# Transposing the backward weights in another order, and an f32 selection product in 32-column groups

## The chip, the cores and the metric

The kernel runs on one core of one Trainium2 chip. The metric is the device time of one execution in microseconds (us), given as the median of several runs. The engines named below are PE (matrix products and transposes; PEld are its weight loads), DVE (vector engine), ACT (scalar engine), POOL (GpSimd) and SP (SyncE, which here only issues DMAs). PE writes to PSUM, which holds eight banks of 2 KB per partition; DVE and ACT copy ("evict") results from there to SBUF.

## The reference

The function is the gradient of a sum of two branches behind a layernorm: a recurrent attention layer with 8 memory rows that are handed from one 32-row segment to the next, and an MLP with squared ReLU. All ten gradients are returned beside the output.

```python
for s in range(n_seg):                       # 64 segments of 32 rows
    h = jnp.concatenate([mem, xs], axis=1)   # 8 memory rows + 32 rows, D = 512
    q, k, v = (jnp.einsum('btd,dhe->bhte', h, W) for W in (Wq, Wk, Wv))   # 32 heads of 128
    scores = jnp.einsum('bhqe,bhke->bhqk', q, k) * scale
    p = _softmax(jnp.where(mask, scores, -1e9))
    o = jnp.einsum('bhqk,bhke->bhqe', p, v)
    o = jnp.einsum('bhte,hed->btd', o, Wo)
    mem = o[:, :M, :].copy()
    outs.append(o[:, M:, :])
# B: h = xn @ w1 + b1; out = relu(h)**2 @ w2 + b2
# out = x + A(xn) + B(xn);  the result is (out, vjp(grad_out) for x, mem0, Wq, Wk, Wv, Wo, w1, b1, w2, b2)
```

The inputs are bf16: x is 1 x 2048 x 512, Wq, Wk and Wv are 512 x 32 x 128, Wo is 32 x 128 x 512, w1 is 512 x 1792.

## The kernel before, in words

The program has four stages: the MLP, forward and backward, with the layernorm (to about 250 us); the forward recurrence (to about 1226 us, with a seam behind it); the backward recurrence (about 1312 to 2435); and the products that make the gradients of Wq, Wk, Wv and Wo (to the end).

In the first three stages nothing is issued in the order of the source. Each stage adds operations to a `_Plan` (L40): an engine or a choice of engines with an estimated duration, the keys that the operation reads and writes, a priority (0 for the recurrence, 1 for work beside it), and a latency. `run` (L100) gives each operation a rank, the longest path of estimated costs to the end, and then simulates the engines: it takes the operation that can start first, prefers a higher rank among those that can start at about the same time, adds `_TURN` (0.095 us) where PE changes between tile forms ("f" full 128x128, "w" 128x32 column groups, "d" 32x32 blocks), and writes out the order found. Every engine then works through its own list in this order, with semaphores between engines. A changed estimate, a new dependency or a changed priority can so move any operation of the stage.

`Stage.bank` (L348) hands out PSUM banks: each kind ("c", "f", "m" forward; "c", "r", "f" backward) is a ring of a fixed number of banks, and an operation that gets a bank depends on whatever used that bank before it in the source.

One segment of the forward recurrence is `chain` (L956): projections q, k, v, scores, softmax, products with v, product with Wo (`wo_part`), and the selection `tm` (L1001), eight bf16 matmuls that pick the memory rows out of `mb` for the next segment. Beside it run the memory rows' own work for each block of four segments (`l_proj`, `l_attn`) and `dw_unit` (L1056), which makes the gradients of w1 and w2 in 14 units of two 128-row chunks; each chunk is evicted into the single buffer `wt` and stored, 28 stores in all, on SP's queue. For w1's gradient the chunk is transposed once more through PSUM back into `wt` before it is stored.

The backward recurrence needs the weights transposed. `turn` (L361) does this for Wq, Wk or Wv in place in 16 groups: eight 128x128 PE transposes into one bank, one eviction of 128x1024. `turn_o` (L377) does it for Wo, also 16 groups, each with two evictions of 128x512. Wq (kind "m", two banks) and Wo (kind "c", four banks) are turned at the end of the forward plan (L1108, L1109), Wv and then Wk at the start of the backward plan (L1374), both with kind "f", two banks, which the memory rows' work of backward also uses.

One segment of the backward recurrence is `chain` (L1298), from segment 63 to 0: the product `gO` of the incoming gradient with Wo, its transposes `gOT`, `dP`, the softmax backward on DVE (L1163 to L1168), then three parts, each a product in 32x32 blocks (`d2`, `d1`, `d0`), an eviction to `dN`, a DVE transpose to `dT` and 64 matmuls of 128x512 (`dh_part`, L1172) with the transposed Wv, Wk and Wq. They add up in `ps_dRA`. DVE or ACT copies this to `R_A` (f32, 128 x 512) in two halves. The selection product `gm` (L1344) adds up the four 32-row groups of `R_A` and keeps the 8 memory rows, transposed: for each 128-column chunk `dc`, `R_A`'s chunk is the stationary operand (128x128, f32) and the constant `sel8` (128x8) the moving one. DVE copies the result into `gT` (L1349), which is the input of the next segment's `gO`. `l_pre` (L1190) makes the memory rows' gradients that `d2` (`gLN`) and `d1` (`dSL`) of a block need; `l_post` follows a block.

The last `l_attn` of forward (b = 15) takes part of its `VM` from SBUF, with four small DMAs issued by ACT (L914).

Of the kernel before, what the change touches and what calls it, by code (L numbers as in the profile page):

```python
# [17 lines left out]
P = 128  # L18
# [7 lines left out]
class _PE(dict):  # L26
    shape = None
# [8 lines left out]
class _Op:  # L36
    __slots__ = ("idx", "cost", "fn", "prio", "deps", "users", "left", "done", "end", "eng", "lat", "shape")


class _Plan:  # L40
# [11 lines left out]

    def add(self, cost, fn, R=(), W=(), prio=1, lat=None):
        o = _Op()
        o.idx = len(self.ops)
        o.cost = cost
# [43 lines left out]
    def run(self):  # L100
# [4 lines left out]
        for o in reversed(ops):  # L105
            c = min(o.cost.values())
            t = 0.0
            for u in o.users:
                same = o.cost.keys() == u.cost.keys() and "SP" not in o.cost
                t = max(t, rank[u.idx] + (0.0 if same else o.lat + _HOP))  # L110
            rank[o.idx] = c + t
        elig = [o for o in ops if o.left == 0]
# [74 lines left out]
def kernel(  # L187
# [152 lines left out]
    class Stage:  # L340


        def __init__(self, plan, pools):
            self.plan = plan
            self.pools = pools
            self.cnt = {k: 0 for k in pools}

        def bank(self, kind, shape, dt, name):  # L348
            n = self.pools[kind][1]
            key = (kind, self.cnt[kind] % n)  # L350
            self.cnt[kind] += 1
            return _Bank(self.pools[kind][0], key, shape, dt, name)

# [6 lines left out]

        def turn(self, kind, nm, reg, key, okey):  # L361

            for g in range(DC * NI // 2):
                dc, i0 = g % DC, 2 * (g // DC)
                blk = reg[:, dc, i0 * JQ * P:(i0 + 2) * JQ * P]
                bk = self.bank(kind, [P, 8, P], BF16, "ps_" + nm)

                def tr(e, blk=blk, bk=bk):
                    src = blk.rearrange("p (i m c) -> p i c m", i=2, c=JQ)
                    for i in range(2):  # L370
                        for c in range(JQ):
                            transpose_to(bk()[:, JQ * i + c, :], src[:, i, c, :])
                self.plan.add(pe(0.46, "f"), tr, [key] if g else [], [bk.key] + ([] if g else [key]), 1)
                self.evict(lambda blk=blk: blk, bk,
                           lambda bk=bk: bk()[:].rearrange("p k d -> p (k d)"), [(okey, g)], 1, {"DVE": 0.85, "ACT": 1.1})

        def turn_o(self, kind, nm, reg, key, okey):  # L377

            for g in range(2 * NI):
# [8 lines left out]
                self.plan.add(pe(0.46, "f"), tr, [key] if g else [], [bk.key] + ([] if g else [key]), 1)  # L388
                for d in range(2):
                    self.evict(lambda blk=blk, d=d0 + d: blk[:, :, d * P:(d + 1) * P].rearrange("p j (a c) -> p j a c", c=JQ), bk,  # L390
                               lambda bk=bk, d=d: bk()[:, d].rearrange("p c (j a) -> p j a c", j=JQ), [(okey, g, d)], 1, EV_B)

# [373 lines left out]
    with tc.tile_pool(name="fw", bufs=1) as fw, \  # L766
# [137 lines left out]
        def l_attn(b):  # L904
# [4 lines left out]
            else:  # L909
# [3 lines left out]
                for j in range(JQ):  # L913
                    sg.dma(lambda j=j: flat(VM)[32 * j + M * n:32 * (j + 1)], lambda j=j: flat(vN)[32 * j:32 * j + M],  # L914
                           [("vN", 0), ("vN", 1)] + ([("VMe", x) for x in range(JQ)] if j == 0 else []),
                           ["VM"] if j == 0 else [("VMx", j)], 0, eng="ACT")
            bk = sg.bank("f", [P, NI, 2 * RL], F32, "ps_scL")
# [138 lines left out]
        def dw_unit(which, u):  # L1056
# [59 lines left out]
    if True:  # L1116
# [181 lines left out]
        def chain(s):  # L1298
# [41 lines left out]
            if s > 0:  # L1340
                p1, v1 = ((s - 1) // SPB) % 2, (s - 1) % SPB
                bm = sg.bank("c", [P, DC, M], F32, "ps_gm")
                for hf in range(2):
                    def gm(e, hf=hf):  # L1344
                        for dc in (2 * hf, 2 * hf + 1):
                            nc.tensor.matmul(bm()[:, dc, :], lhsT=R_A[:, dc * P:(dc + 1) * P], rhs=sel8[:],  # L1346
                                             start=True, stop=True, skip_group_check=True)
                    A(pe(0.46, "f"), gm, [("R_A", hf)], [bm.key], 0)
                A({"DVE": 0.19}, lambda e: V.tensor_copy(gT[p1][:, :, RA * v1:RA * v1 + M], bm()[:]),  # L1349
# [211 lines left out]
```

## Time and profile before

| what | us |
|---|---|
| median of 3 runs | 3028.18 (3020.16 to 3029.71) |
| the profiled execution | 3031.71 |
| its span | 3029.9 |
| PE busy | 2788.3 |
| DVE busy | 1558.8 |
| ACT busy | 959.2 |
| POOL busy | 352.8 |
| stage 250 to 1226, forward recurrence | 976 |
| stage 1226 to 1312, the seam | 86 |
| stage 1312 to 2435, backward recurrence from the second segment | 1123 |

The profile is of one execution. "Busy" is the time in which at least one instruction of the engine is under way; matmuls overlap, and their ends are modelled. A row of a timeline or a group reads: start, duration, engine, line, operation, output<-inputs, shapes, number of instructions; in brackets the idle time of the engine just before it and what ended it. In a group's row the three durations are least, median and largest, in ns. The granted clock is the share of PE's full clock that was passed to it. A helper's line (L311, L315, L317, L359) stands for many places, so the tile's name tells them apart: `WA` holds Wq, Wk and Wv, `WB` Wo, `PA` the inputs of a segment, called `hA` forward and `gT` backward.

### The profile page before, as it was taken

Reading aid. Unit: us, or ns where it says so; the run is one execution under the profiler, and the core shown is the slowest. Engines: PE = TensorE matmul, PEld = TensorE weight load, DVE = VectorE, ACT = ScalarE, POOL = GpSimd, SP = SyncE. Lnnn points to the kernel's source line nnn. Section 1 sums busy time; section 2 is a strip of 40 time slices with the busy share of each in tenths; the row PEclk is TensorE's granted clock in tenths of the full one; section 3 lists DMA queues with packets and bytes.
Section 4 is the critical chain, followed back from the end, with each engine's and each line's share of the span. In section 5 each row is a group of like instructions: output and inputs, shape, how many; then the busy total and the mean of one; then the engine's idle time right before and its main releaser. Section 6 shows DMA issues by size and latency. Waiting matters only on the chain.

```text
span 3029.9 us, 129853 instructions
## 1 busy us (share of the span) xinstructions
PE 2788.3 (92%) x58168; PEld 1601.9 (53%) x58168; DVE 1558.8 (51%) x3378; ACT 959.2 (32%) x1978; POOL 352.8 (12%) x608
## 2 busy tenths in 40 slices
PE   8998999999999899888898898989899899999999
PEld 6664555555555555655555555555555544444444
DVE  5544555555555555655555555655655521332322
ACT  4324444444454444422333333333333310000000
POOL 1111111111111111100000000000000001211111
PEclk9999999999999999999999999999999999999999
DMA  6648665566555665456767777777777789788861
GB/s 208 219 141 228 167 170 174 170 174 179 161 153 164 159 173 173 130 139 187 206 201 204 206 204 196 220 209 200 208 214 214 197 288 310 235 256 277 248 182 44
DMA packets 551933, 589.96 MB, mean 195 GB/s; under 512 B 237445, under 2 KB 353078, under 8 KB 549198
## 3 DMA queue, kind: packets, MB, share of 16 engines
q1 hardware_dynamic: 537342, 530.72, 61.3%
q0 software_dynamic: 13968, 50.87, 4.9%
q8 instruction: 454, 7.44, 1.1%
q14 instruction: 105, 0.86, 0.1%
q10 hardware_dynamic: 64, 0.07, 0.0%
HBM read 283.32 MB, written 262.68 MB: 180 GB/s over the span
## 4 chain that ended last, share of the span: by engine, by line
PE 55%; issue 19%; DMA 10%; DVE 8%; SPq 3%; ACT 3%; POOL 2%; DVEq 0%; ACTq 0%; POOLq 0%
PE ps_dRA L1179 9%; PE ps_d L449 6%; PE ps_q L413 4%; PE ps_RA L861 3%; PE ps_h L620 3%; PE ps_k L413 3%; PE ps_dRL L1179 3%; SPq L359 3%; PE ps_gO L413 2%; PE ps_v L413 2%; PE ps_dw L1071 2%; PE ps_gm L1346 2%; PE ps_gxb L648 2%; PE ps_B L648 2%; PE ps_o L449 1%
## 5 line engine op out<-in xcount | busy, mean ns | idle before, releaser
L1179 PE MATMUL ps_dRA<-WA,dT 128*32 128x512 bf16 x6144 | 375.4, 385 | 11.6 <-issue 8.0
L1508 PE MATMUL ps_gw<-WA,WB 128*128 128x512 bf16 x1536 | 332.3, 379 | 0.6 <-DVE gwo L315 0.6
L413 PEld LDWEIGHTS <-PA 128*32 128x32 bf16 x8192 | 205.5, 98 | 231.6 <-DVE PA L1009 25.4
L397 DVE STREAM_TRANSPOSE dT<-dN 128x512 bf16<-128x512 bf16 x384 | 256.3, 693 | 99.8 <-ACT dN L317 98.5
L1508 PEld LDWEIGHTS <-WB 128*128 128x128 bf16 x1896 | 185.4, 98 | 225.0 <-issue 1.7
L317 ACT CAST dN<-ps_d 128x512 bf16<-128x512 f32 x357 | 199.7, 588 | 290.6 <-PE ps_d L449 252.3
L315 DVE CAST gwo<-ps_gw 128x512 bf16<-128x512 f32 x64 | 39.7, 682 | 402.9 <-PE ps_gw L1508 268.7
L1179 PEld LDWEIGHTS <-dT 128*32 128x32 bf16 x6144 | 156.3, 97 | 169.5 <-issue 23.6
L317 ACT CAST gwo<-ps_gw 128x512 bf16<-128x512 f32 x64 | 32.9, 599 | 515.4 <-PE ps_gw L1508 385.5
L1289 POOL COPY bVT<-VR 128x1024 bf16<-128x1024 bf16 x64 | 66.7, 1042 | 970.6 <-PE ps_dP L1311 873.0
L413 PE MATMUL ps_q<-WA,PA 128*32 128x512 bf16 x2048 | 157.4, 384 | 8.3 <-DVE PA L1009 8.3
L449 PEld LDWEIGHTS <-PB 32*32 32x32 bf16 x8192 | 119.0, 92 | 81.2 <-issue 48.6
L413 PE MATMUL ps_k<-WA,PA 128*32 128x512 bf16 x2048 | 156.3, 382 | 0.3 <-DVE PA L1009 0.3
L413 PE MATMUL ps_gO<-WB,PA 128*32 128x512 bf16 x2048 | 140.4, 421 | 12.7 <-DVE PA L1349 12.1
L315 DVE CAST kN<-ps_k 128x512 bf16<-128x512 f32 x112 | 77.4, 691 | 143.8 <-PE ps_k L413 143.8
L861 PE MATMUL ps_RA<-WB,OT 128*32 128x256 bf16 x4096 | 126.7, 273 | 13.0 <-DVE OT L397 9.5
L413 PE MATMUL ps_v<-WA,PA 128*32 128x512 bf16 x2048 | 130.6, 383 | 0.0
L1071 PE MATMUL ps_dw<-sx,anT 128*128 128x512 bf16 x448 | 121.8, 385 | 6.6 <-DMA sx<-in_grad_out_dram 6.1
L317 ACT CAST qN<-ps_q 128x512 bf16<-128x512 f32 x115 | 67.2, 587 | 185.3 <-PE ps_q L413 160.2
L861 PEld LDWEIGHTS <-OT 128*32 128x32 bf16 x4096 | 102.2, 97 | 39.9 <-DVE OT L397 28.6
L842 POOL TENSOR_TENSOR P<-P,rsA 128x320 bf16<-128x320 bf16 x64 | 46.3, 723 | 589.1 <-DVE rsA L837 269.1
L317 ACT CAST gON<-ps_gO 128x512 bf16<-128x512 f32 x79 | 44.9, 587 | 202.1 <-PE ps_gO L413 199.0
(304 smaller groups left out, 5024.1 us busy)
## 6 DMA issues: line engine op xcount, KB each, us to landing
S_GN<-dN SPq DMA_DIRECT2D x192, 256.0 KB
WA<-S_GN SPq DMA_DIRECT2D x160, 256.0 KB
S_Q<-qN SPq DMA_DIRECT2D x64, 256.0 KB
S_K<-kN SPq DMA_DIRECT2D x64, 256.0 KB
S_V<-vN SPq DMA_DIRECT2D x64, 256.0 KB
S_ON<-oN SPq DMA_DIRECT2D x64, 256.0 KB
bqN<-S_Q SPq DMA_DIRECT2D x64, 256.0 KB
bkN<-S_K SPq DMA_DIRECT2D x64, 256.0 KB
```

The source lines that it names most:

```text
L315: nc.vector.tensor_copy(out, in_)
L317: nc.scalar.copy(out, in_)
L359: self.plan.add({eng: cost}, lambda e: q.dma_start(out_f(), in_f()), R, W, prio, lat)
L397: self.plan.add({"DVE": 0.70}, lambda e, x=x: nc.vector.transpose(dst[:, x, :, :], src[:, x, :].rearrange("p i (a c) -> p i c a", c=JQ)), ...
L413: nc.tensor.matmul(bk()[32 * j:32 * (j + 1), :], lhsT=win(dc), rhs=Wt(dc, c0), start=(dc == 0), stop=(dc == DC - 1), tile_position=(0, 32 ...
L449: nc.tensor.matmul(bk()[32 * j:32 * j + m, k * P:(k + 1) * P], lhsT=lf(j, i), rhs=rf(j, i), start=(k == 0 and x == 0), stop=(x == n - 1), ...
L620: nc.tensor.matmul(bk()[:, x, :], lhsT=Wt[:, dc, fc * P:(fc + 1) * P], rhs=In[:, dc, :], start=(dc == 0), stop=(dc == DC - 1), skip_group_ ...
L648: nc.tensor.matmul(bk()[:], lhsT=src[z][:, fc, rc * P:(rc + 1) * P], rhs=Wt[:, fc, :], start=(fc == 0 and first), stop=(fc == FC - 1))
L861: nc.tensor.matmul(bk()[32 * c:32 * (c + 1), :], lhsT=OTt[:, i, j, :], rhs=Wo[:, JQ * i + j, dh * DH:(dh + 1) * DH], start=(i == 0 and j < ...
L1071: nc.tensor.matmul(bks[x]()[:], lhsT=anT[x][:, c, :], rhs=sx[z][:], start=(c == 0), stop=(c == TC - 1))
L1179: nc.tensor.matmul(bk()[32 * j:32 * (j + 1), :], lhsT=XT[:, i, j, :], rhs=wtf(t, JQ * i + j), start=(first and i == 0), stop=(last and i = ...
L1508: nc.tensor.matmul(bks[n]()[:], lhsT=HNc[:, rc, dc * P:(dc + 1) * P], rhs=gns[y][:, hf * 512:(hf + 1) * 512], start=(y == 0), stop=(y == N ...
```

## The change

- The f32 selection product (L1343): each 128-column chunk is made by four matmuls with 32 stationary columns, each in its own column group of PE, so 16 matmuls where there were 4. Its estimate in the plan goes from 0.46 with form "f" to 0.4 with form "w", for each half.
- The end of forward turns the first 8 groups of Wv where it turned all of Wq; the turning of Wo gets 40 us added to its rank (`lift`).
- The start of backward turns the other 8 groups of Wv, then Wk, then Wq. `rings` gives the turns banks of their own: c4, f1, c2, c3, and for Wq c4 and f1; the memory rows' work has f0 alone until the first segment's chain is planned, and the chain c0 to c3. A planned operation on an engine "X" that does not exist, 8 us long and with no instruction, writes the key of Wo, so that the plan starts `gO` no sooner.
- The estimates of evictions in `turn` and `turn_o` change.
- The four DMAs of the last `VM` go from ACT's queue to POOL's, and the 28 stores of `dw_unit` from SP's to POOL's.

```diff
-            rank[o.idx] = c + t
+            rank[o.idx] = c + t + o.lift
...
-            n = self.pools[kind][1]
-            key = (kind, self.cnt[kind] % n)
-            self.cnt[kind] += 1
-            return _Bank(self.pools[kind][0], key, shape, dt, name)
+            ring = self.rings.get(kind) or [(kind, x) for x in range(self.pools[kind][1])]
+            key = ring[self.cnt.get(kind, 0) % len(ring)]
+            self.cnt[kind] = self.cnt.get(kind, 0) + 1
+            return _Bank(self.pools[key[0]][0], key, shape, dt, name)
...
-        def turn(self, kind, nm, reg, key, okey):
+        def turn(self, kind, nm, reg, key, okey, g0=0, g1=DC * NI // 2):
-            for g in range(DC * NI // 2):
+            for g in range(g0, g1):
...
-                           lambda bk=bk: bk()[:].rearrange("p k d -> p (k d)"), [(okey, g)], 1, {"DVE": 0.85, "ACT": 1.1})
+                           lambda bk=bk: bk()[:].rearrange("p k d -> p (k d)"), [(okey, g)], 1, {"DVE": 0.7, "ACT": 1.0})
...
-        def turn_o(self, kind, nm, reg, key, okey):
+        def turn_o(self, kind, nm, reg, key, okey, lift=0.0):
...
-                               lambda bk=bk, d=d: bk()[:, d].rearrange("p c (j a) -> p j a c", j=JQ), [(okey, g, d)], 1, EV_B)
+                               lambda bk=bk, d=d: bk()[:, d].rearrange("p c (j a) -> p j a c", j=JQ), [(okey, g, d)], 1, {"DVE": 0.61, "ACT": 0.59})
...
-                           ["VM"] if j == 0 else [("VMx", j)], 0, eng="ACT")
+                           ["VM"] if j == 0 else [("VMx", j)], 0, eng="POOL")
...
-                    sg.dma(lambda fc=fc: out_9[fc * P:(fc + 1) * P, :], lambda: wt[:], ["wt"], [])
+                    sg.put(lambda fc=fc: out_9[fc * P:(fc + 1) * P, :], lambda: wt[:], ["wt"], [])
...
-                    sg.dma(lambda fc=fc: out_7.rearrange("(c p) f -> p c f", p=P)[:, :, fc * P:(fc + 1) * P],
+                    sg.put(lambda fc=fc: out_7.rearrange("(c p) f -> p c f", p=P)[:, :, fc * P:(fc + 1) * P],
...
-        sg.turn("m", "Wq", Wqkv[0], ("WA", 0), "WqT")
-        sg.turn_o("c", "Wo", WB[:], "WB", "WoT")
+        sg.turn("m", "Wv", Wqkv[2], ("WA", 2), "WvT", 0, 8)
+        sg.turn_o("c", "Wo", WB[:], "WB", "WoT", 40.0)
...
-                            nc.tensor.matmul(bm()[:, dc, :], lhsT=R_A[:, dc * P:(dc + 1) * P], rhs=sel8[:],
-                                             start=True, stop=True, skip_group_check=True)
-                    A(pe(0.46, "f"), gm, [("R_A", hf)], [bm.key], 0)
+                            for j in range(JQ):
+                                nc.tensor.matmul(q_(bm(), j)[:, dc, :], lhsT=R_A[:, dc * P + 32 * j:dc * P + 32 * (j + 1)],
+                                                 rhs=sel8[:], start=(dc == 0), stop=True, tile_position=(0, 32 * j),
+                                                 skip_group_check=True)
+                    A(pe(0.4, "w"), gm, [("R_A", hf)], [bm.key], 0)
...
-        for t, nm in ((2, "Wv"), (1, "Wk")):
-            sg.turn("f", nm, Wqkv[t], nm, (t, "WT"))
+        A({"X": 8.0}, lambda e: None, [], ["WB"])
+        sg.rings = {"t": [("c", 4), ("f", 1), ("c", 2), ("c", 3)], "f": [("f", 0)], "c": [("c", x) for x in range(4)]}
+        sg.turn("t", "Wv", Wqkv[2], "Wv", (2, "WT"), 8)
+        sg.turn("t", "Wk", Wqkv[1], "Wk", (1, "WT"))
+        sg.rings["t"] = [("c", 4), ("f", 1)]
+        sg.turn("t", "Wq", Wqkv[0], "Wq", (0, "WT"))
...
                 chain(s)
+                sg.rings = {}
                 if s > 0:
```

More of the change, by code (lines that the diff above doesn't have):

```diff
@@ L36 @@
 class _Op:
-    __slots__ = ("idx", "cost", "fn", "prio", "deps", "users", "left", "done", "end", "eng", "lat", "shape")
+    __slots__ = ("idx", "cost", "fn", "prio", "deps", "users", "left", "done", "end", "eng", "lat", "shape", "lift")
 class _Plan:
@@ L51, in __init__, with add @@
         self.keep = keep
-    def add(self, cost, fn, R=(), W=(), prio=1, lat=None):
+    def add(self, cost, fn, R=(), W=(), prio=1, lat=None, lift=0.0):
         o = _Op()
+        o.lift = lift
         o.idx = len(self.ops)
@@ L345, in __init__ @@
             self.pools = pools
-            self.cnt = {k: 0 for k in pools}
+            self.cnt = {}
+            self.rings = {}
         def bank(self, kind, shape, dt, name):
-            n = self.pools[kind][1]
-            key = (kind, self.cnt[kind] % n)
-            self.cnt[kind] += 1
-            return _Bank(self.pools[kind][0], key, shape, dt, name)
+            ring = self.rings.get(kind) or [(kind, x) for x in range(self.pools[kind][1])]
+            key = ring[self.cnt.get(kind, 0) % len(ring)]
+            self.cnt[kind] = self.cnt.get(kind, 0) + 1
+            return _Bank(self.pools[key[0]][0], key, shape, dt, name)
         def put(self, out_f, in_f, R, W, prio=1, lat=3.5, cost=0.5):
@@ L372, in tr @@
                             transpose_to(bk()[:, JQ * i + c, :], src[:, i, c, :])
-                self.plan.add(pe(0.46, "f"), tr, [key] if g else [], [bk.key] + ([] if g else [key]), 1)
+                self.plan.add(pe(0.46, "f"), tr, [key] if g > g0 else [], [bk.key] + ([] if g > g0 else [key]), 1)
                 self.evict(lambda blk=blk: blk, bk,
-                           lambda bk=bk: bk()[:].rearrange("p k d -> p (k d)"), [(okey, g)], 1, {"DVE": 0.85, "ACT": 1.1})
-        def turn_o(self, kind, nm, reg, key, okey):
+                           lambda bk=bk: bk()[:].rearrange("p k d -> p (k d)"), [(okey, g)], 1, {"DVE": 0.7, "ACT": 1.0})
+        def turn_o(self, kind, nm, reg, key, okey, lift=0.0):
             for g in range(2 * NI):
@@ L387, in tr @@
                             transpose_to(bk()[:, d, c, :], blk[:, c, (d0 + d) * P:(d0 + d + 1) * P])
-                self.plan.add(pe(0.46, "f"), tr, [key] if g else [], [bk.key] + ([] if g else [key]), 1)
+                self.plan.add(pe(0.46, "f"), tr, [key] if g else [], [bk.key] + ([] if g else [key]), 1, lift=lift)
                 for d in range(2):
                     self.evict(lambda blk=blk, d=d0 + d: blk[:, :, d * P:(d + 1) * P].rearrange("p j (a c) -> p j a c", c=JQ), bk,
-                               lambda bk=bk, d=d: bk()[:, d].rearrange("p c (j a) -> p j a c", j=JQ), [(okey, g, d)], 1, EV_B)
+                               lambda bk=bk, d=d: bk()[:, d].rearrange("p c (j a) -> p j a c", j=JQ), [(okey, g, d)], 1, {"DVE": 0.61, "ACT": 0.59})
         def sq_T(self, src, sk, dst, dk, prio):
```

## The prediction

> **What bounds the kernel now.** I read the busy times by stage first, then the TensorE (PE) rows of the seam between the two recurrences, then the groups of the selection product.
>
> The busy table by stage (columns: stretch, then per engine busy us and instructions, granted clock, DMA share, GB/s):
>
> ```profile
> 250.00:1226.00 976.00, 900.39 (x22752) 531.14 (x22751) 551.49 (x1188) 432.42 (x956) 114.55 (x215) 0.99 0.60 170
> 1226.00:1312.00 86.00, 71.01 (x1547) 54.34 (x1548) 61.04 (x112) 33.63 (x55) 10.68 (x19) 0.94 0.51 120
> 1312.00:2435.00 1123.00, 1002.06 (x28715) 596.04 (x28714) 652.58 (x1299) 357.83 (x660) 90.29 (x138) 0.97 0.73 202
> 1237.00:1245.00 8.00, 5.01 (x152) 4.53 (x150) 6.16 (x14) 5.39 (x10) 3.30 (x7) 0.79 0.26 67
> 1264.00:1274.00 10.00, 6.70 (x67) 5.59 (x67) 6.70 (x13) 2.34 (x4) 0.40 (x1) 0.66 0.67 196
> ```
>
> PE is the busiest engine everywhere. The seam, 1226 to 1312, is the loosest: 15 of 86 us idle, and in two stretches PE runs at a granted clock of 0.79 and 0.66. The backward recurrence, 1312 to 2435, has 63 segments of 17.8 us, each a chain of waits that ends in the selection product `ps_gm`. The timeline of the seam:
>
> ```profile
> 1235.41 3.24 ACTq L359 DMA_DIRECT2D VM<-vN  x4
> 1236.96 0.49 DVE L830 TENSOR_TENSOR stA<-ps_sc,mxA 128x320 f32<-128x320 f32 x1
> 1240.14 0.49 ACT L832 ACTIVATE P<-stA 128x320 bf16<-128x320 f32 x1
> ...
> 1240.30 1.05 PE L311 MATMUL ps_Wq<-ident,WA 128*128 128x128 bf16 x16 [2.99 <-ACT WA L317]
> 1266.95 6.27 PE L311 MATMUL ps_Wv<-ident,WA 128*128 128x128 bf16 x56 [3.02 <-ACT WB L317]
> 1285.48 10.37 DVE L315 COPY WA<-ps_Wk 128x1024 bf16<-128x1024 bf16 x15
> 1295.12 1.91 PE L413 MATMUL ps_gL<-WB,PB 128*32 128x512 bf16 x32
> 1303.90 0.22 PE L449 MATMUL ps_d<-bqLN,dSL 32*8 32x128 bf16 x4 [1.96 <-DVE dSL L1168]
> ```
>
> ACT issues four DMAs for 3.24 us, so the last forward softmax, whose input is there at 1237.45, gets its exponential at 1240.14 and PE stands 2.99 us. At 1263.93 PE waits 3.02 us for the last Wo eviction before the first backward transpose. Then 15 Wk evictions run on VectorE (DVE) alone, 0.69 us each, PE in step with them; `gL`, allotted the same two banks after all 32 groups, starts at 1295.12, and `d1` waits for what follows from it. The selection product, with its forward counterpart:
>
> ```profile
> L1346 PEld LDWEIGHTS ps_gm<-sel,R_A x504: 186/192/338, 1311.7 to 2434.5; 128*128 128x128 f32 x168
> L1346 PE MATMUL ps_gm<-sel,R_A x504: 256/256/382, 1311.7 to 2434.5; 128*128 128x8 f32 x168
> L1004 PE MATMUL ps_mem<-sel,PB x504: 169/172/196, 254.2 to 1226.2; 128*32 128x16 bf16 x168
> ...
> 1639.44 0.97 PEld L1346 LDWEIGHTS ps_gm<-sel,R_A 128*128 128x128 f32 x8 [0.42 <-ACT R_A L317]
> 1639.44 1.06 PE L1346 MATMUL ps_gm<-sel,R_A 128*128 128x8 f32 x8
> 1226.17 0.12 PEld L1004 LDWEIGHTS <-PB 128*32 128x32 bf16 x8 [0.89 <-DVE PB L869]
> 1226.17 0.22 PE L1004 MATMUL ps_mem<-sel,PB 128*32 128x16 bf16 x8 [0.72 <-DVE PB L869]
> ```
>
> 504 records over 63 segments are 8 per segment: an f32 matmul leaves two. Eight loads in 0.97 us, each 0.192, start (0.97-0.192)/7 = 0.111 us apart; the narrow bf16 loads (0.12-0.093)/7 = 4 ns apart.
>
> **Part 1, the f32 product in 32-column groups.** Removed per segment: 4 matmuls of 128x128 (8 records). Added: 16 of 128x32 (32 records), and PE stays in the 128x32 tile form of its neighbours. In 33 of the 63 segments both halves run back to back, 1.06 us from first start to last end, and the copy to `gT` follows in 0.04 us. In the other 30 the halves are apart, and the copy starts 0.59 us after the second ends, since DVE is first at a 0.69 us cast of `dLN`; there an earlier end of up to 0.59 us is worth nothing.
> No row shows a narrow f32 load. Lower end: the bf16 spacing of 4 ns. Upper end: the wide spacing of 111 ns, if width bought nothing. Against the upper end: bf16 loads of 128 columns start 56 ns apart (16 transposes in 1.08 us, each 0.219: 0.86/15), those of 32 columns 4 ns. An f32 record takes twice the wide bf16 one (111 against 56); the forward product's two rounds of four tiles start 39 ns apart, so I take a round of four f32 records at about 60 ns. A half has 16 records, four rounds: 0.24 us where it was 4 x 0.111 = 0.44. Both halves: 2 x 0.24 + 0.24 for the last record to end = 0.72 against 1.06, so -0.34. The change of form goes too: a 512-column matmul of L1179 is followed by a matmul of its own form 0.205 us later, by `ps_gm` 0.309 later, so -0.10. Sum: 33 x 0.44 = -14 us, and 30 x 0 behind DVE's cast. Ends: at 4 ns, 32 x 0.004 + 0.24 = 0.37, so 33 x 0.79 = -26 (and a little more if the copy is planned ahead of the cast); at 111 ns, 3.79 us, so 33 x (2.73 - 0.10) = +87, and 30 x (1.78+0.24-0.61-0.59 = 0.82) = +25, +112 in all.
> The Trainium skill (TensorE: Matmul & The Clock Gate, Part 1, "Wait — 56ns, not 53.3ns?") says that matmul starts never come closer than about 25 ns however small they are. The trace differs where the matmuls lie in different column groups: `ps_mem` puts eight starts into (0.22-0.17) = 0.05 us, some 7 ns apart. By the rule 16 records would take 0.40 us a half, hardly less than now, and the part would be worth 33 x (1.06-1.04+0.10) = -4 us.
>
> **Part 2, the seam.** Forward does 8 groups of Wv where it did 16 of Wq; backward does 8 of Wv, 16 of Wk, 16 of Wq where it did 32: 64 groups with Wo both times, 0.46 us of PE each at full clock, so their PE and eviction work is unchanged. What can go is what stands around them, by the rows of idle PE: 2.99 (ACT's DMA issues go to GpSimd (POOL), idle from 1227 until 1239.63; four at 0.635 end by 1238 and `VM` is read at 1243; `S_HNA` and the normalising of P, at 1242.7, are behind them); 1.5 in three waits of Wo's transposes for evictions, as six Wq groups leave that stretch; 3.02, as backward's first banks are others than Wo's; 3.4 of waits in the two-bank ring, now four banks with eviction costs of 0.7 and 1.0 that match the rows (0.69 on DVE, 1.01 on ACT), so that ACT takes a share; 1.96 before `d1`, as `gL` has bank f0 for itself. That is 12.9 us. Lost clock: 5.01 us busy at 0.79 is 1.1, 6.70 at 0.66 is 2.3. Together 16 us. The other end is 3, ACT's queue alone. What takes their place: the eight-us planned hold on WB lets `gO` begin no sooner than some 17 groups (8/0.46) into backward; 16 Wq groups, first needed by `d0`'s product, now compete with the first chain for DVE (23 groups left, at 0.69); and Wo needs 32 evictions on two engines, 32/(1/0.68+1/0.59) = 10 us, whatever PE does. I take -10: about 10 us before 1266.95 and nothing behind, since backward takes on 8 groups more (3.7 us) and gains about as much. The hold itself issues no instruction; lift and rings only change the order.
>
> **Part 3, 28 gradient stores of `dw` from SP to POOL.** SP loses 28 issues of 0.42 = 12 us and what the loads of `sx` waited behind them; POOL gains 14 x 0.54 (rows of 1 KB, as out_6's) + 14 x 0.75 (256-byte pieces, as out_3's) = 18 us, in a stage where it is busy 115 of 976. Behind them on POOL stand the normalising of P and the adds to `obA`; P has a segment's time, 15 us, so this costs nothing; were that gone, each would cost 0.75. `wt` is one buffer: its next eviction waits for the store, on ACT or DVE. Now these waits are 18.0 us in 8 cases; stores wait up to 7 us in SP's queue and land 2.3 to 3.6 us after issue. On POOL a store of this size took 5.6 to land in the last stage, a small one 1.7. Ends: -9 (half of the waits) and +15 (14 re-uses within a unit, each 2 us later, half on the chain). I take -2, since the queue wait saved is about the landing lost. The order of the whole forward and backward plan shifts with any cost; I give that no sign.
>
> **Sum.** -14 - 10 - 2 = -26. The profiled execution took 3031.71 (span 3029.9 and 1.8 around it), 3.5 above the median of 3028.18: 3031.7 - 26 = 3005.7 against that execution, 3002 against the median.
>
> **Rivals.**
> (B) Narrow records follow one another at 25 to 28 ns: loads pass singly, in proportion to width, 111 x 32/128 = 28 ns; 32 x 0.028 + 0.24 = 1.13 us; part 1 leaves 33 x (0.07-0.10) = -1, sum -13, 3015. For it: the spacing of 111 looks like pure load time. Against: the 4 ns of bf16. Chance 0.17, of which 0.05 for a floor on the spacing whatever the width, which at 25 ns gives 33 x (1.04-1.06-0.10) = -4 and 3012. The Trainium skill's page named above states such a floor.
> (C) The wait at the seam is only moved: `d0` stands for Wq's last groups on two banks. Part 2 leaves -1: 3011. For it: Wq is needed 20 us after `gO`; against: 23 groups at 0.46 are 11 us. Chance 0.10.
> (D) Slower: a narrow f32 record takes as long as half a wide one or more. It turns part 1 into a loss; the total passes +9 from about 50 ns (32 x 0.050 + 0.24 = 1.84, 33 x 0.68 = +22, less 12). At 56 ns it is 33 x 0.87 - 12 = +17, 3045; at 111, +100, 3128. For it: 16 pairs replace 4; against: the bf16 rows. Chance 0.08.
> (E) The stores on POOL hold `wt` and ACT behind it: +15 to +36 on the forward recurrence (14 x 2.6), with the other parts -9 to +12: 3019 to 3040. For it: the 5.6 us above. Against: POOL is idle 88% there. Chance 0.10.
> The forecast keeps 0.55, by itself 2988 to 3014.
>
> **Range and chances.** No change, to a measurement of this kernel, is within 0.3%, 9 us: 3019 to 3037. Faster: forecast 0.52, B 0.12, C 0.08, E 0.02: 0.74. Same: 0.03 + 0.04 + 0.02 + 0.05 = 0.14, slower: D 0.08, E 0.03, B 0.01 = 0.12. Low end 2982: 4-ns records (-26) with 16 from the seam and a little from part 3. High end 3024: B with C and part 3 at zero or slightly worse; D and most of E lie beyond.
>
> **What will show it.** `ps_gm` first start to last end near 0.7 us in back-to-back segments and 17.4 us a segment (record spacing under 20 ns bears me out, 28 is B, over 50 is D); no idle of 3 us on PE in the seam, the clock at 1 there, and the first `R_A` some 10 us sooner after the last forward product; waits of ACT and DVE for `wt` no longer than 18 us. I am wrong if the segment length does not move while `ps_gm` shrinks (the recurrence is then bound by other PE work or by DVE), or if Wq's evictions delay `d0`.

## The result, and the profile after

The changed kernel takes 3014.63 us (median; 3000.14 to 3023.17) where the kernel before, run beside it, takes 3031.33 (3020.16 to 3044.29): a ratio of 0.9939, 95% interval 0.9923 to 0.9954, that is 18.5 us less (14 to 23). The ratio is taken over all runs; the two medians alone lie 16.7 us apart. The profiled execution took 3020.57, with a span of 3018.8.

The busy table by stage, after (the columns of the first table of before):

```profile
250.00:1226.00 976.00, 905.58 (x22993) 535.78 (x22984) 554.71 (x1197) 445.59 (x998) 134.77 (x247) 0.99 0.60 170
1226.00:1312.00 86.00, 73.91 (x1684) 58.19 (x1687) 61.58 (x114) 34.57 (x57) 12.56 (x22) 0.88 0.48 133
1312.00:2435.00 1123.00, 980.14 (x30264) 568.60 (x30259) 650.28 (x1296) 357.45 (x662) 88.75 (x136) 0.96 0.74 203
1246.00:1264.00 18.00, 11.10 (x97) 9.42 (x95) 10.19 (x20) 1.82 (x4) 4.59 (x7) 0.60 0.35 82
```

The stretches are cut at the times of before; the changed kernel reaches the backward recurrence 10.9 us sooner (the first copy to `gT` ends at 1302.0, before at 1312.9), so two other marks serve better: the last `ps_mem`, where forward ends, and the copies to `gT`, where each backward segment ends. The last column is the link that part 1 shortens: from the end of the second copy to `R_A` to the start of the first `gO` matmul, with the selection product and the copy to `gT` between them. From these marks (us):

| | first to last `ps_mem` | last `ps_mem` to first `gT` | the two together | first to last `gT` (62 segments) | `R_A` complete to first `gO`, mean |
|---|---|---|---|---|---|
| before | 972.0 | 86.7 | 1058.8 | 1122.1 | 1.345 |
| after | 958.7 | 87.5 | 1046.2 | 1120.5 | 1.067 |

Two things stand out. The gain in this pair of profiles lies ahead of the backward recurrence. And in the backward recurrence the link that part 1 shortens did get shorter, by 0.28 us a segment, 17 us over 62 segments, while the stage got only 1.6 shorter.

The seam after, PE's timeline:

```profile
1229.27 1.01 PE L1073 MATMUL ps_dw<-sx,anT 128*128 128x512 bf16 x2 [3.56 <-DMA sx<-S_XN]
...
1245.89 0.59 PE L1073 MATMUL ps_dw<-sx,anT 128*128 128x512 bf16 x2
...
1248.74 0.61 PE L312 MATMUL ps_Wv<-ident,WA 128*128 128x128 bf16 x8 [1.06 <-DVE wt L316]
1250.13 1.01 PE L312 MATMUL ps_Wv<-ident,WA 128*128 128x128 bf16 x8 [0.78 <-DVE WA L316]
...
1261.75 5.66 PE L312 MATMUL ps_Wv<-ident,WA 128*128 128x128 bf16 x56 [0.78 <-DVE WA L316]
...
1278.03 1.91 PE L415 MATMUL ps_gO<-WB,PA 128*32 128x512 bf16 x32
```

The last unit of `dw`, which before was over earlier, is still at work in the seam (`ps_dw` until 1246). Its two banks are the ring "m" that the first 8 groups of Wv use, so these come behind it, one at a time, each behind an eviction on DVE (0.78 us of idle PE per group), and the granted clock in 1246 to 1264 is 0.60. The second of the two banks comes free late because its eviction into `wt` waits 4.1 us on ACT, to 1251.3, until the store of the chunk before, now issued by POOL, has left `wt`.

The selection product after, its tile's rows and then one segment of the timeline:

```profile
L1349 PEld LDWEIGHTS ps_gm<-sel,R_A x2016: 106/112/158, 1301.0 to 2422.1; 128*32 128x32 f32 x184
L1349 PE MATMUL ps_gm<-sel,R_A x2016: 169/176/223, 1301.2 to 2422.1; 128*32 128x8 f32 x184
```

```profile
1334.39 0.77 PE L1349 MATMUL ps_gm<-sel,R_A 128*32 128x8 f32 x32 [0.19 <-ACT R_A L318]
```

A record is one instruction in the profile, here a matmul or a weight load. The matmuls leave 32 a segment as counted in the prediction, 0.77 us from the first start to the last end as the commonest case, where it was 1.06. How long the engines of this tile sat idle for DVE's copy of the second half of `R_A` (us, times), before and after:

```profile
  DVE R_A L315: 22.4, 14
...
  DVE R_A L316: 37.2, 50
```

In the commonest case the two copies to `R_A` end 0.46 us apart, before and after. A wide half of the product took 0.47 us to the start of the next and filled that time; a narrow half is over sooner, and in 59 of the 63 segments its second half starts within 0.07 us of DVE's copy (before in 28). So 0.77 is 0.46 of waiting for `R_A` and 0.31 of the second half.

The waits of PE and its weight loads in 1312 to 2435 that no semaphore ended ("issue"), in total us, times and longest. Before:

```profile
PE ps_d L449 <- issue: 20.9, 21, 2.9
...
PE ps_dRA L1179 <- issue: 6.0, 8, 1.4
...
PE ps_gm L1346 <- issue: 1.5, 2, 1.2
...
PEld L449 <- issue: 54.5, 80, 3.1
...
PEld L1179 <- issue: 23.9, 57, 1.9
```

After:

```profile
PE ps_d L451 <- issue: 22.1, 22, 4.2
...
PE ps_dRA L1181 <- issue: 10.0, 15, 1.6
...
PE ps_gm L1349 <- issue: 4.8, 5, 1.8
...
PEld L451 <- issue: 57.4, 79, 4.4
PEld L1181 <- issue: 39.9, 91, 2.0
```

Here is what the prediction had left out. Counting from the trace only stretches over 0.15 us in which neither PE nor its weight loads ran and that no semaphore ended, the 62 segments have 45 of them before, 42.5 us in sum, and 65 after, 61.2 us. The queue that carries instructions tells what they are: in these segments it moved 225 packets of 16 KB for PE's 57,400 records before and 236 for 60,404 after, a packet per 256 records, and every one of the 45 and the 65 waits ends 1.0 to 1.8 us after the end of such a packet; a random moment lies so in 16 to 17% of cases, and of the 116 and 112 waits that a semaphore ended 17 and 12% do. PE runs out of instructions. The largest group of these waits, 28 of the 65 with 32 of the 61 us, stands ahead of the products in 32x32 blocks (L451), which use up 128 records in about 1 us; but before it had 26 with 29 us. Of the 20 further waits 10 stand at the matmuls of `dh_part` (L1181, 18 where there were 8). One of the waits lies in the middle of the selection product itself:

```profile
1639.77 0.24 PE L1349 MATMUL ps_gm<-sel,R_A 128*32 128x8 f32 x7
1641.80 0.38 PE L1349 MATMUL ps_gm<-sel,R_A 128*32 128x8 f32 x25 [1.79 <-issue]
...
1642.33 0.19 DVE L1353 CAST PA<-ps_gm 128x32 bf16<-128x32 f32 x1 [1.55 <-PE ps_gm L1349]
```

Seven records had come, the other 25 came 1.8 us later, at a packet that ended at 1640.30.

### The profile page after: what moved, and what is told of

Read it like the earlier page. It is cut to its first block, busy times and chain, and to the rows that moved or that the text cites. A ratio compares the mean times of both kernels' runs of the same rounds, so it can differ in the third digit from the quotient of the medians.

```text
span 3018.8 us, 132985 instructions
## 1 busy us (share of the span) xinstructions
PE 2761.1 (91%) x59680; PEld 1575.5 (52%) x59680; DVE 1551.3 (51%) x3367; ACT 967.4 (32%) x2013; POOL 372.8 (12%) x640
## 3 DMA queue, kind: packets, MB, share of 16 engines
q1 hardware_dynamic: 527934, 527.05, 61.2%
## 4 chain that ended last, share of the span: by engine, by line
PE 64%; issue 11%; DMA 10%; DVE 9%; SPq 2%; ACT 2%; POOL 1%; DVEq 0%; ACTq 0%; POOLq 0%
PE ps_gw L1517 11%; PE ps_dRA L1181 7%; PE ps_d L451 6%; PE ps_q L415 4%; PE ps_k L415 3%; PE ps_RA L863 3%; PE ps_h L622 3%; PE ps_gO L415 3%; PE ps_dw L1073 2%; PE ps_v L415 2%; PE ps_dRL L1181 2%; PE ps_B L650 2%; SPq L361 2%; PE ps_gxb L650 2%; DMA dLN<-S_GNL 1%
## 5 line engine op out<-in xcount | busy, mean ns | idle before, releaser
L1181 PE MATMUL ps_dRA<-WA,dT 128*32 128x512 bf16 x6144 | 382.5, 388 | 13.9 <-issue 10.2
L1181 PEld LDWEIGHTS <-dT 128*32 128x32 bf16 x6144 | 158.5, 98 | 175.7 <-issue 34.4
L451 PEld LDWEIGHTS <-PB 32*32 32x32 bf16 x8192 | 119.1, 92 | 79.3 <-issue 45.9
L415 PE MATMUL ps_gO<-WB,PA 128*32 128x512 bf16 x2048 | 138.3, 414 | 16.8 <-DVE PA L1353 15.3
L1181 PE MATMUL ps_dRL<-WA,LT 128*32 128x512 bf16 x1536 | 108.9, 387 | 2.3 <-issue 1.2
```

The source lines that it names most:

```text
L415: nc.tensor.matmul(bk()[32 * j:32 * (j + 1), :], lhsT=win(dc), rhs=Wt(dc, c0), start=(dc == 0), stop=(dc == DC - 1), tile_position=(0, 32 ...
L451: nc.tensor.matmul(bk()[32 * j:32 * j + m, k * P:(k + 1) * P], lhsT=lf(j, i), rhs=rf(j, i), start=(k == 0 and x == 0), stop=(x == n - 1), ...
L1181: nc.tensor.matmul(bk()[32 * j:32 * (j + 1), :], lhsT=XT[:, i, j, :], rhs=wtf(t, JQ * i + j), start=(first and i == 0), stop=(last and i = ...
```

## The experiments

Theory after the result: part 2 gives its 10 us; part 1 shortens the chain as worked out, and gives most of it back, since its 24 further pairs of load and matmul a segment (48 records) have to be fetched. Rivals: part 1's gain is eaten by DVE's cast ahead of the copy; by the shifted plan; or the stores take it. In what follows "forward and seam" and "backward" are the third and fourth columns of the table above. One profile scatters: the five kernels with the forward plan of before gave 1055.8 to 1060.4 for forward and seam, mean 1058.1; the three that share the 64-column product in the change's backward plan gave 1102.6 to 1124.3 for backward. Single profiles of backward are therefore read by the parts that the theory names, and the stage by means over kernels. Kernels are compared in time only with the kernel before, or with each other, on the same chip.

**The parts alone.** The 32-column product put into the kernel before, with its new estimate:

```diff
-    nc.tensor.matmul(bm()[:, dc, :], lhsT=R_A[:, dc * P:(dc + 1) * P], rhs=sel8[:], ...)
-A(pe(0.46, "f"), gm, [("R_A", hf)], [bm.key], 0)
+    for j in range(JQ):
+        nc.tensor.matmul(q_(bm(), j)[:, dc, :], lhsT=R_A[:, dc * P + 32 * j:dc * P + 32 * (j + 1)], ...)
+A(pe(0.4, "w"), gm, [("R_A", hf)], [bm.key], 0)
```

> The kernel before with the 32-column selection product alone, its estimate in the plan included. Theory 1 (the product is on the chain, and the profile after hides its worth because other edits cost the backward recurrence as much): 0.28 us a segment sooner from R_A to gO, 63 segments, 12 to 18 us faster, 3013 to 3019 against 3031. Theory 2 (the time saved in the product is given back inside the segment, before R_A): ps_gm shrinks as it did, the segment stays at 18.1 us, and the whole moves by less than 5 us.

The same matmuls, but `A(pe(0.46, "f"), ...)` kept, so that every queue has the order of before:

> The 32-column product is issued, but the plan keeps its old estimate (0.46, full form), so every queue keeps the order of the kernel before. Theory 1: 10 to 18 us faster, as the whole edit. Theory 2 splits here: if the order is what gives the time back, this one is 10 us or more faster than before and than the whole edit; if the hardware does (PE, DVE or a DMA binds the segment elsewhere), it stays within 5 us of before although R_A to gO shrinks by 0.2 us or more.

The 28 stores alone, `sg.dma(` to `sg.put(` in `dw_unit`:

> The kernel before with the 28 stores of dw on POOL alone, planned as on POOL. The profile after has its forward recurrence 13 us shorter. Theory 3 (the stores on SP's queue hold wt or the loads of sx, and this is where the change gained): 10 to 16 us faster, first to last ps_mem from 972 to about 959 us. Rival (it comes from the seam edits, which let dw work slip behind the last segment, so that forward only looks shorter and the seam longer): within 4 us of before.

The seam alone: the changed kernel with the wide product and with the stores on SP:

> The whole change without the 32-column product and without the stores on POOL: turns, banks, the hold, estimates, VM on POOL. My prediction gave this 10 us. Theory 4 (the prediction): 8 to 12 us faster, last ps_mem to first ps_gm 75 to 78 us instead of 86. Rival (the profile after has the seam at 87 us, so the edit is worth nothing by itself and the gain is all in forward): within 4 us of before.

| | ratio to before | 95% | forward and seam | backward | `R_A` to `gO` | waits for instructions in backward |
|---|---|---|---|---|---|---|
| product, new estimate | 0.9966 | 0.9949 to 0.9982 | 1056.7 | 1117.6 | 1.082 | 65.5 |
| product, old order | 0.9975 | 0.9959 to 0.9992 | 1060.4 | 1124.7 | 1.006 | 62.1 |
| stores | 0.9984 | 0.9963 to 1.0005 | 1055.1 | 1126.0 | 1.322 | 45.9 |
| seam | 0.9953 | 0.9930 to 0.9977 | 1056.4 | 1123.5 | 1.326 | 40.2 |

In time (before: 3043.7 on this chip) the product alone is worth 10 us (5.5 to 15.5), or 8 with the order of before, and the seam 14 (7 to 21); the stores 5 with an interval that takes in nothing. So the shifted plan is not what ate part 1: with the order of before the product gains no more. There the link shortened by 0.34 us a segment, 21 us in all, the waits for instructions grew by 19.6, and the profiled stage did not get shorter (1124.7 against 1122.1). The seam's profile showed less than its time: 1056.4, only 1.7 under the mean of the old plan. The clock does not account for it: in that profile 34 us of forward ran at a granted clock of 0.5 where before had 21, but none of the seam where before had 10, so 34 against 31 over both. Why this one profile shows less than the time stays open; it lies within the scatter of single profiles.

**The change without a part.** The changed kernel once more, and with the wide product put back (the diff above, reversed):

> The changed kernel itself, unaltered, as the base for the three beside it. About 0.994 of before. Its backward recurrence (first to last copy of ps_gm, 62 segments) near 1120 us, and waits of PE that no semaphore ends (the profile's issue) near 61 us there.

> The changed kernel with the wide selection product and its old estimate. Theory A (what the narrow product saves on the chain, 0.28 us x 62 = 17 us, is eaten by PE waiting for its instructions, of which the narrow product has 24 matmuls and 24 loads more in each segment): issue waits of PE back near 42 us, the recurrence within 5 us of that of the changed kernel, the whole 2 to 8 us slower. Theory B (the product is worth its chain time, and the seam and the stores are worth little): 14 to 18 us slower than the changed kernel.

On one chip they took 3015.67 and 3020.87, before 3025.93: ratios 0.9962 (0.9946 to 0.9978) and 0.9985 (0.9968 to 1.0003). The product is worth 5 us within the change (4.8 by the means, give or take 4.5). `R_A` to `gO` is 1.102 and 1.353, the waits for instructions 66.4 and 36.5: 0.25 x 62 = 15.6 us gained on the chain, 30 us more of waits, and the backward recurrence at 1120.8 and 1118.9. Not all of the waits can lie on the chain, or the stage would have grown by 14.

Over all profiles (more records, below, left out): with the wide product backward took 1122.6 (mean of four), `R_A` to `gO` 1.336, waits for instructions 41.3; with 32 columns 1120.8 (five), 1.065 and 63.9; with 64 columns, below, 1114.8 (four), 1.138 and 53.7. So 32 columns shorten the link by 0.271 x 62 = 16.8 us, add 22.6 of waits, and leave 1.8.

How much of the waits lies on the chain can be read from the segments, since all 14 profiles have the same 62. Each segment is compared with the mean of the same segment over the profiles, with the length of the link and the time at a granted clock of 0.5 fitted beside the waits. A segment with 1 us more of waits for instructions is then 0.54 us longer (95%: 0.38 to 0.70), one with 1 us more on the link 0.58 (0.30 to 0.89). So about half of the waits lie on the chain, and the estimate for the stage is 16.8 x 0.58 = 10 us gained and 22.6 x 0.54 = 12 lost. The clock is a rival for part of such comparisons: 1 us more at 0.5 makes a segment 0.40 longer, and the stage had 78.5, 73.7 and 65.7 us of it on average with the wide product, 32 and 64 columns. It favours the narrow products, so it cannot be what took back the gain of 32 columns; but of the 6.0 us between 32 and 64 columns it makes up some 3.

With the stores back on SP:

> The changed kernel with the 28 stores of dw on SP's queue as before. Against the changed kernel: if the seam edits carry the gain ahead of the backward recurrence, the stretch from the first ps_mem to the first ps_gm copy stays near 1049 us and the whole within 4 us; if the stores carry it (they let the last unit of dw slip into the seam, where 24 of its matmuls now stand), the stretch goes to 1055 to 1059 us and the whole is 5 to 10 us slower, while the seam alone shrinks to 75 to 79 us, as it did without them.

0.9944 (0.9923 to 0.9964), and 1049.5 for forward and seam, where the kernels with the change's own forward plan (the changed kernel twice, the wide product put back, and the 64-column product below) gave 1046.2, 1050.0, 1055.5 and 1045.9, mean 1049.4: within the change no worth of the stores can be seen. They do change the plan. With them on SP the seam is as the prediction saw it. Its row of the busy table from 1227, and PE's turning of Wv:

```profile
1227.00:1305.00 78.00, 70.06 (x1596) 54.16 (x1600) 57.01 (x107) 37.99 (x62) 12.66 (x23) 0.96 0.53 135
```

```profile
1244.05 1.04 PE L312 MATMUL ps_Wv<-ident,WA 128*128 128x128 bf16 x8
...
1261.46 1.05 PE L312 MATMUL ps_Wv<-ident,WA 128*128 128x128 bf16 x16 [1.51 <-DVE WA L316]
...
1265.12 4.91 PE L312 MATMUL ps_Wv<-ident,WA 128*128 128x128 bf16 x56 [0.78 <-DVE WA L316]
```

Five of the first eight groups of Wv are turned ahead of those of Wo or between them (1244 to 1260). The seam takes 77.5 instead of 87.5, at a clock of 0.96, and forward 972.0 instead of 958.7. The last unit of `dw` is work that lies in forward or in the seam, as the plan has it: before it ends at 1224.6, ahead of the last `ps_mem`; with the stores on SP 11 us behind it (1238.5), in the changed kernel 32 us behind it (1246.5).

**Fewer records for the same product.** The changed kernel with two groups of 64 columns instead of four of 32, so 8 matmuls a segment instead of 16:

```diff
-for j in range(JQ):
-    nc.tensor.matmul(q_(bm(), j)[:, dc, :], lhsT=R_A[:, dc * P + 32 * j:dc * P + 32 * (j + 1)],
-                     ..., tile_position=(0, 32 * j), ...)
+for j in range(2):
+    nc.tensor.matmul(bm()[64 * j:64 * (j + 1), dc, :], lhsT=R_A[:, dc * P + 64 * j:dc * P + 64 * (j + 1)],
+                     ..., tile_position=(0, 64 * j), ...)
```

> The changed kernel with the selection product in two groups of 64 columns: 8 matmuls a chunk pair instead of 16, so 16 PE rows fewer in a half, 32 in a segment; plan untouched. Theory A: issue waits of PE fall from 61 to about 50 us, R_A to gO grows by 0.1 us a segment (6 us) at most, and the whole is 2 to 8 us faster than the changed kernel. Theory B: only the chain counts, so it is 3 to 8 us slower.

The product's rows, and then the waits in 1312 to 2435:

```profile
L1349 PEld LDWEIGHTS ps_gm<-sel,R_A x1008: 132/138/232, 1302.1 to 2405.1; 128*64 128x64 f32 x168
L1349 PE MATMUL ps_gm<-sel,R_A x1008: 169/203/277, 1302.1 to 2405.1; 128*64 128x8 f32 x168
```

```profile
PE ps_gm L1349 <- issue: 0.7, 1, 0.7
...
PEld L451 <- issue: 46.8, 80, 2.9
PEld L1181 <- issue: 33.5, 54, 3.6
```

3009.46 against 3015.67 of the changed kernel on this chip (ratio to before 0.9940, 0.9917 to 0.9962; the difference of the means is 7.1, give or take 6.4; the mean granted clock of these runs is the same, 0.978). Each record is longer, the product less short (0.86 us in the commonest case, `R_A` to `gO` 1.157), yet the kernel is the faster one, with 48.3 us of waits for instructions where the changed kernel had 61.2 and 66.4. If only the product's own duration counted, it would be the slower one. The same in the kernel before, with the old estimate and order:

> The kernel before with the selection product in two groups of 64 columns, its old estimate and so the old order of every queue; beside gm_issue only the width of the groups differs. Theory A (instruction loading eats the narrow product's gain): 8 more matmuls and loads a segment than before instead of 24; issue waits of PE in the backward recurrence near 48 us against gm_issue's 62, the recurrence at 1105 to 1112 us against its 1125, the whole 10 to 18 us faster than before. If the chain alone counted, it would be no faster than gm_issue.

0.9966 (0.9939 to 0.9993) where 32 columns had 0.9975 (0.9959 to 0.9992): in time no difference that these intervals can tell. Its profile has 53.4 us of waits (62.1 with 32 columns) and a backward recurrence of 1115.1 (1124.7).

**More records, off the chain.** The kernel before, with 24 matmuls with 8 moving columns, on weights that are zero, added to each product in 32x32 blocks of the memory rows' work in `l_post`; over a block of four segments that makes 24 pairs a segment, as many as the narrow product adds:

```diff
+for n in range(24):
+    j = n % JQ
+    nc.tensor.matmul(bks[half]()[32 * j:32 * (j + 1), 0:8],
+                     lhsT=ident[32 * j:32 * (j + 1), 32 * ((j + 1) % JQ):32 * ((j + 1) % JQ) + 32],
+                     rhs=q_(lx, j)[:, 0, 0:8], start=False, stop=False, tile_position=(32 * j, 32 * j), ...)
```

> The kernel before with 24 more matmuls of zeros, 32x32 by 8 columns, in each own product of l_post: 96 per block, 24 per segment, as many PE rows as the narrow selection product adds, but beside the recurrence and not in its chain. Outputs do not change. Their own time on PE is 96 x 7 ns = 0.7 us a block, 11 us in all at most. Theory A: issue waits of PE rise from 42 to about 60 us and the whole is 10 to 25 us slower. If instruction loading is not what limits, the issue waits stay at 42 and the whole is 0 to 8 us slower.

The page's row of the instruction queue (packets, MB, share; before it has 454, the changed kernel 466), and then the waits in 1312 to 2435:

```profile
q8 instruction: 466, 7.63, 1.1%
```

```profile
PE ps_dL L1274 <- issue: 10.4, 5, 3.1
...
PEld L449 <- issue: 52.5, 77, 2.6
...
PEld L1179 <- issue: 32.0, 59, 2.6
```

1.0051 (1.0034 to 1.0069), 15.4 us slower (10 to 21). The recurrence's chain has nothing new on it (`R_A` to `gO` 1.372), the queue carries as many packets as in the changed kernel, and the waits for instructions rise from 42.5 to 63.9 us. One reservation: the added matmuls take time on PE as well, 14 us by the distances from one of their starts to the next, waits among them included. So the run shows what 24 pairs a segment cost beside the chain, not how that splits between fetching and executing; that fetching has a share is shown by the waits.

**Pulling `dw` out of the seam.** `DLW` makes the projection of segment 4u + 16 wait for unit u of `dw`. For the last two of the 14 units that is segment 64 and 68; there are none, so these two are due at no segment. On the 64-column kernel:

```diff
-        DLW = {4 * u + 16: [("dw", u)] for u in range(FC)}
+        DLW = {4 * u + 11: [("dw", u)] for u in range(FC)}
```

and `4 * u + 8` in a second kernel.

> A candidate for a better version: the changed kernel with the product in 64-column groups, and each unit of dw due five segments earlier, so that the last is done before segment 63 and leaves the two banks to the turns of Wv in time. If the late dw unit is what makes the seam 87 us, the seam goes to 75 to 78 us and forward grows by the dw work it takes back, 5 to 9 us: 3 to 7 us faster than 64 columns alone (0.994 of before), so about 0.992. If dw work only fills gaps wherever it stands, 0.994.

> The same with each unit of dw due eight segments earlier. If forward has room for dw work anywhere, as early_dw or 2 us better; if the earlier due times push dw work in front of the chain, forward grows by 5 us or more against early_dw and the whole is slower than it.

Ratios 0.9890 (0.9858 to 0.9922) and 0.9922 (0.9895 to 0.9950). The first is the fastest version of all, 3009.89 on a chip where before takes 3041.04. Its seam, the row of the busy table from 1220 and PE's timeline:

```profile
1220.00:1293.00 73.00, 65.54 (x1550) 51.14 (x1553) 55.08 (x103) 39.25 (x62) 12.67 (x23) 0.98 0.56 133
```

```profile
1228.62 0.61 PE L312 MATMUL ps_Wv<-ident,WA 128*128 128x128 bf16 x8
...
1229.77 0.64 PE L312 MATMUL ps_Wv<-ident,WA 128*128 128x128 bf16 x8
...
1268.84 1.91 PE L415 MATMUL ps_gO<-WB,PA 128*32 128x512 bf16 x32
```

No `ps_dw` is left there, Wv is begun at 1228.6 instead of 1248.7, the clock is at 0.98, and `gO` starts at 1268.8. The seam takes 72.4 and 72.0 in the two, forward and seam 1038.7 and 1039.4, some 10 us under the change's 1049.4. No run has these two kernels beside the plain 64-column one on the same chip, so what the due times alone are worth in time is not measured. That the second is 10 us slower than the first (give or take 4.5) shows behind the seam: 1124.3 against 1117.3 in backward, 62.2 us of waits for instructions against 50.7, with the same number of records; at the 0.54 found above these 11.5 us are 6 of the 7. Where a packet begins depends on how many records went before; that this moved the waits onto or off the chain is argued, not shown.

## Why the prediction was right, and where it was not

The direction and the size class were right; the sum said -26, measured were -18.5 (-14 to -23), and the absolute 3002 was lower still by 3, as it was set against a median of 3028.18 that further runs put at 3031.33.

- **Part 1, -14: the link shortens, but the term is mis-sized.** The step that failed is "33 x 0.44 = -14 us": it priced the edit by the product's length and left the 24 added pairs without a price. What was not in the sum is the fetching of 48 more records a segment: 19 to 30 us more waits of PE, about half of them on the chain, so that the part is worth 5 (within the change) to 10 us (alone), where the link from `R_A` to `gO` became 17 us shorter over 62 segments. The prediction's own sign of failure, "the segment length does not move while `ps_gm` shrinks", is what the profile shows: 1120.5 / 62 = 18.07 us, before 18.10 (the 17.8 of the prediction divides the stage by 63, but 62 segments lie between the first and the last copy). Its explanation there, other PE work or DVE, misses the instruction waits.
- **The length and the link, partly by luck.** That 0.77 us comes near the 0.72 of the sum is luck. A round of four records, taken at 60 ns, is 32 from one record of a column group to its next (52 at the first), the next group's record 7 behind; two halves that follow each other at once took 0.44 and 0.47 us in the two segments that have them. The other 0.3 us is the wait for the second half of `R_A`, which the sum did not have. The split into 33 and 30 segments was misread too: before, the halves are apart in some 10 segments, not 30, and of the 30 copies to `gT` that start over 0.1 us behind the product 12 are 0.59 us late or more, the other 18 0.11 to 0.47. The 33 gained 11.8 us on the link for the 14 forecast, and the 30, put at nothing, gained 5.6; only the 12 gained little, 1.4. The change of tile form went as worked out: behind a 512-column matmul of L1181 the 32-column product starts 0.205 us later, the 64-column one 0.309 like the wide one; but where `R_A` is what the product waits for, this time is not on the link.
- **Part 2, -10: right in size, not in place.** Forward and seam together fell by 8.7 (means of four and five profiles), by 14 (7 to 21) in the time of the seam alone. But the signs in the seam were wrong. "No idle of 3 us on PE in the seam" and "the clock at 1 there": there is one of 3.56, for a load of `sx`, and the clock falls to 0.60. "The first `R_A` some 10 us sooner after the last forward product": not sooner, it is the last forward product that came 11.7 us sooner. I had not followed the last unit of `dw`: it went from forward into the seam, with the stores on POOL furthest, and Wv's first groups waited for its banks. With the stores on SP the seam comes out near the forecast (77.5 us, clock 0.96), at the same total. That the total held although the gain came at another place was not foreseen, and is in so far luck.
- The four DMAs of `VM` on POOL did what was said. The last softmax after, in order of DVE, POOL and ACT:

```profile
1224.97 0.48 DVE L832 TENSOR_TENSOR stA<-ps_sc,mxA 128x320 f32<-128x320 f32 x1
...
1223.67 2.08 POOL L361 DMA_DIRECT2D VM<-vN  x4 [8.47 <-DVE hN L316]
...
1225.54 0.47 ACT L834 ACTIVATE P<-stA 128x320 bf16<-128x320 f32 x1 [1.72 <-issue]
```

The exponential starts 0.09 us after its input is there; before it was 2.7 us late behind ACT's issues.

- **Part 3, -2: right within what can be told**, nothing to be seen inside the change, -5 (-11 to +1.5) alone. The waits of `wt` for its store after, and the landing time:

```profile
  DMA out_dram<-wt: 13.3, 8
...
DMA to landing us min/median/max: 2.2/3.3/5.9
```

13.3 us in 8 cases instead of 18.0, as "the queue wait saved is about the landing lost" has it.
- **The rivals.** B and its floor of 25 ns fell: 32 records take 0.44 and 0.47 us in the two segments where both halves are ready close together, not the 1.04 to 1.13 of the rival. The Trainium skill's statement (TensorE: Matmul & The Clock Gate, Part 1, "Wait — 56ns, not 53.3ns?") that starts never come closer than about 25 ns does not hold here across column groups, 7 ns for f32 as for bf16; within one group the 32 ns agree with it. D fell with B. C fell: after, PE waits only 0.23 us for Wq's last eviction ahead of the last matmuls of `d0`'s part (1299.87). E fell by the 13.3 us.

## What to carry to other kernels

A matmul split into narrow pieces costs instructions, and on a long unrolled stream they are not free: before pricing such an edit by the length of the operation, look for waits of PE that no semaphore ended, compare their ends with the packets of the instruction queue, and give each further record a price from them. Of two ways to shorten an operation on the chain, take the one with fewer instructions first; here two groups of 64 beat four of 32 in the full change (7.1 us, give or take 6.4) although each segment's product is longer; in the kernel before no difference could be told. And an operation that waits for its own inputs, as the second half here for `R_A`, gains no more than its last part. And where a stage's order is planned, ask for each changed cost which piece of unforced work can slip over the stage's end, and give it a due time there.

## What the runs showed of the hardware that was not expected

- PE waits for its own instructions. In 1122 us of backward recurrence with 57,400 records it stood 36 to 46 us in this way in the kernels with the wide product, with 60,400 records 61 to 66, always until 1.0 to 1.8 us after a 16 KB packet of the instruction queue. The Trainium skill (Runtime: NRT & Kernel Launch, "Instruction fetch mechanics") says that instructions come in such blocks of 256, and that crossing from one to the next is mostly hidden; the block size agrees, that it is hidden does not.
- f32 matmuls in 32-column groups: load 112 ns, matmul 176, the next group's record 7 ns behind, the same group's next 32; in 64-column groups 138 and 203 ns.
